# Two-bank PSUM tiles split into one tile per bank, casts moved off ScalarE, a transpose left out, late row tiles routed one by one

## The chip, the cores and the metric

The kernel runs on one core of one Trainium2 chip. The time is the device time of one execution in microseconds (us). Engines are named as the profile names them: PE (TensorE, matmul), PEld (its weight load), DVE (VectorE), ACT (ScalarE), POOL (GpSimd), SP (SyncE, which here only issues DMAs).

## The reference

A gated linear attention over 4 batches, 8 heads, 768 steps and head size 48 is followed by a mixture of 8 experts over the 3072 rows that come out of it. Cut to what is computed:

```python
for t in range(S):
    state = alpha[:, :, t, :, None] * state + einsum('bhd,bhe->bhde', k[:, :, t], v[:, :, t])
    y[:, :, t] = einsum('bhd,bhde->bhe', q[:, :, t], state)
x = y.transpose(0, 2, 1, 3).reshape(3072, 384)
compute = x @ w_skip > 0
e_idx = argmax(x @ w_gate);  gate = softmax(x @ w_gate)[e_idx]
for e in range(8):                      # w1[e]: 384 x 1024, w2[e]: 1024 x 384
    out[rows of e] = x + gate * (relu(x @ w1[e]) @ w2[e])     # only where compute
```

## The kernel before, in words

**Attention.** The rows are cut into 24 tiles of 128, numbered i; two batches go side by side, so i = 2 x chunk + batch within a pair, with 6 chunks per batch. Per tile, DVE scans the decays (L232, L240), POOL multiplies q and k by them (L236, L242), PE makes the scores (L257), DVE copies the masked diagonal blocks (L266) and ACT the others (L272). PE adds the products with v and with the carried state in ps_y (L313); a tiny ACT copy, the fence "spot" (L344), orders two halves of these. ACT copies the result out (turn_y, L351); PE turns it into rows and logits (L359), ACT copies the rows (L365), DVE reduces the logits (L370). PE transposes k (turn_k, L280), ACT copies that, and outer (L293) adds k times v to the state, which DVE scales (L300) and ACT keeps (L305). The last chunk of a batch has no outer, since no chunk follows.

**Routing.** Row tiles are routed in groups. `route` finds the expert and the gate with a string of small DVE instructions and an exp on ACT; ACT rounds the gate into `vals` (L410), POOL subtracts for the low part (L411). `rank` counts rows before each row by two matmuls with the constant matrices tri and one_b (L417, L419), `place` makes slot numbers (L433 to L436). A one-hot of a tile (`one_hot`, L445, 256 columns) times `mv` (`marks`, L450) adds row numbers and gates to a table in PSUM (L458), from which rows are gathered by number.

**Late tiles.** For tiles 18 to 23 the rows of expert 0 do not go through DRAM: one-hots of expert 0's slots (`mine`, L440) select them by matmul (`late_rows`, L509) from two-part splits of the tile (`late_split`, L500, L501) straight into three PSUM banks; `early_turn` (L515) adds the rows gathered earlier, `first_turn` (L523, L525) copies the sum out as xh and xl.

**Experts.** Every matmul is made of two-part operands (hi and lo). Weights come by DMA (L536) as `raw`; ACT casts hi (L556), DVE or POOL subtract for lo (L560). `up(e, g)`, g = 0 to 3, is 18 matmuls into one PSUM bank of three that are taken in turn (ps_y's two and ps_g); ACT makes hh (L633) and DVE hl (L634) from it. `down(e, j)`, j = 0, 1, is 24 matmuls (L645) into ps_v or ps_c; DVE makes o (L649), POOL scatters it by row number (L651). Behind the first down stands `turn(e + 1)`: three transposes into each bank of ps_s (L609), ACT's xh (L611) and DVE's xl (L612) for each. POOL gathers the rows of later experts (L478). A guard checks alpha's range with two ACT instructions (`over`, L597) per down, for eight parts of alpha.

**Order.** The order on each engine is that of the program text (a manual schedule); the framework adds the semaphores from the tiles that instructions read and write. Instructions on one engine run in order. w1's hi and lo have one buffer each, raw has three.

## Time and profile before

| | |
|---|---|
| median of 3 runs (lowest, highest) | 324.94 us (324.41, 328.82) |
| profiled execution, device time | 327.61 us |
| its span in the trace | 325.9 us |
| PE busy | 270.8 us, 83% of the span |
| DVE, POOL, ACT busy | 198.2, 179.2, 159.5 us |
| mean granted PE clock | 0.954 |

The span is what the trace covers; the rest of the device time lies around it. Attention fills the first 136 us, the first up of expert 0 starts at 143.9, the last down ends at 319.3. A row of a timeline gives the start, the length, the engine and line, the operation, what it writes and reads, how many instructions it merges, and in brackets how long the engine was idle before and which instruction ended that. The granted clock is a share of 2.4 GHz.

### The profile page before, as it was taken

What the parts mean: (1) busy time and instruction counts of PE and PEld (TensorE: products, weight loads), DVE (VectorE), ACT (ScalarE), POOL (GpSimd) and SP (SyncE); (2) the same over time, 40 slices, a digit from 0 to 9 for tenths busy, and PEclk for the clock granted to TensorE, in tenths of its full rate; (3) what the DMA queues carried; (4) which work ended last, traced back from release to release, by engine and by line L of the source; (5) the groups of instructions that cost most, each with busy time, mean ns of one, the idle gap of its engine ahead of it and who ended that gap; (6) DMA issues with size and microseconds to landing.
All of it is one profiled execution on the core that took longest, in us unless ns stands there. A gap on an engine that the chain in (4) does not pass through costs nothing.

```text
span 325.9 us, 9204 instructions
## 1 busy us (share of the span) xinstructions
PE 270.8 (83%) x3766; PEld 250.9 (77%) x3766; DVE 198.2 (61%) x362; ACT 159.5 (49%) x338; POOL 179.2 (55%) x199
## 2 busy tenths in 40 slices
PE   0798999898889799893989886878897888898891
PEld 0687987787778688683989886878887888898791
DVE  5765788778778886574555534535438456563720
ACT  3144554545456545612447385495495554453500
POOL 4545564648778978761574552643736265542611
PEclk9998999889999979996799997997999999999998
DMA  7987688969888964713372539449259557250001
GB/s 255 353 309 227 189 271 294 299 209 330 286 250 258 318 202 148 246 54 109 114 251 70 211 90 392 144 162 394 84 186 350 193 171 251 65 195 26 10 12 34
DMA packets 32178, 65.30 MB, mean 200 GB/s; under 512 B 4469, under 2 KB 11535, under 8 KB 32128
## 3 DMA queue, kind: packets, MB, share of 16 engines
q1 hardware_dynamic: 29952, 59.59, 54.9%
q0 software_dynamic: 2176, 5.05, 4.8%
q8 instruction: 31, 0.51, 0.6%
q14 instruction: 19, 0.16, 0.2%
HBM read 56.99 MB, written 8.85 MB: 202 GB/s over the span
## 4 chain that ended last, share of the span: by engine, by line
PE 59%; DVE 13%; ACT 8%; POOL 7%; issue 7%; DMA 3%; SPq 1%; POOLq 0%; DVEq 0%; ACTq 0%
PE ps_y L629 12%; PE ps_c L645 10%; PE ps_y L313 7%; PE ps_v L645 6%; PE ps_g L629 5%; PE ps_s L257 5%; PE ps_g L359 3%; PE ps_k L280 3%; ACT over L597 3%; DVE sfx L240 2%; PE ps_v L458 2%; PE ps_v L293 2%; ACT w1h L556 2%; PE ps_s L609 2%; DVE hl L634 2%
## 5 line engine op out<-in xcount | busy, mean ns | idle before, releaser
L257 PE MATMUL ps_s<-qka 64*64 64x128 f32 (+1 forms) x768 | 33.5, 270 | 11.1 <-DVE qka L242 7.8
L313 PE MATMUL ps_y<-st,vt 64*48 64x128 f32 (+1 forms) x768 | 36.7, 260 | 6.6 <-ACT spot L344 6.1
L560 POOL TENSOR_TENSOR w1l<-raw,w1h 128x512 fp32r<-128x512 f32 x24 | 31.3, 1305 | 17.0 <-ACT w1h L556 13.5
L629 PE MATMUL ps_y<-xh,w1h 128*128 128x240 f32 x132 | 25.3, 300 | 17.1 <-DVE hl L634 16.8
L242 POOL TENSOR_TENSOR qka<-qka,sfx 128x512 f32<-128x512 f32 x23 | 29.4, 1279 | 17.6 <-DVE sfx L240 12.8
L236 POOL TENSOR_TENSOR qka<-qka,pfx 128x512 f32<-128x512 f32 x24 | 26.3, 1095 | 21.1 <-DVE pfx L232 7.9
L651 POOL DMA_INDIRECT out_dram<-o,ids x16 | 17.6, 1098 | 36.9 <-DVE o L649 31.7
L257 PEld LDWEIGHTS ps_s<-qka 64*64 64x64 f32 x768 | 27.0, 143 | 12.4 <-POOL st L160 7.8
L560 POOL TENSOR_TENSOR w2l<-raw,w2h 128x512 fp32r<-128x512 f32 x16 | 21.2, 1327 | 27.1 <-ACT w2h L556 25.9
L629 PEld LDWEIGHTS ps_y<-xh,w1h 128*128 128x128 f32 x132 | 20.4, 205 | 18.8 <-DVE hl L634 18.4
L313 PEld LDWEIGHTS ps_y<-st,vt 64*48 64x48 f32 x768 | 26.8, 129 | 8.9 <-ACT spot L344 7.1
L272 ACT COPY st<-ps_s 64x512 f32<-64x512 f32 x24 | 13.9, 579 | 36.8 <-DVE st L266 30.4
L633 ACT ACTIVATE hh<-ps_y 128x480 fp32r<-128x480 f32 x22 | 12.5, 570 | 38.9 <-PE ps_y L629 35.7
L634 DVE SCALAR_TENSOR_TENSOR hl<-ps_y,hh 128x480 fp32r<-128x480 f32 x22 | 14.4, 652 | 28.1 <-ACT hh L633 28.1
L560 DVE TENSOR_TENSOR w2l<-raw,w2h 128x512 fp32r<-128x512 f32 x32 | 29.3, 935 | 2.8 <-ACT w2h L556 2.2
L232 DVE TENSOR_TENSOR_SCAN pfx<-qka,ps_c 128x527 f32<-128x527 f32 x24 | 29.6, 1233 | 2.2 <-DMA qka<-in_qka_dram 2.2
L240 DVE TENSOR_TENSOR_SCAN sfx<-qka,ps_c 128x525 f32<-128x525 f32 x24 | 29.7, 1238 | 0.3
L266 DVE COPY_PREDICATED st<-mask,ps_s 128x512 f32<-128x512 uint8 x24 | 17.5, 731 | 17.7 <-PE ps_s L257 16.2
L478 POOL DMA_INDIRECT xr<-out_dram,ids x18 | 20.0, 1110 | 13.4 <-DVE gates L495 7.7
L556 ACT CAST w1h<-raw 128x512 fp32r<-128x512 f32 x48 | 27.3, 619 | 0.0
L556 ACT CAST w2h<-raw 128x512 fp32r<-128x512 f32 x48 | 27.1, 616 | 0.0
L629 PE MATMUL ps_y<-xh,w1l 128*128 128x240 f32 x132 | 24.3, 293 | 0.0
(143 smaller groups left out, 711.8 us busy)
## 6 DMA issues: line engine op xcount, KB each, us to landing
raw<-in_w_dram SPq DMA_DIRECT2D x64, 384.0 KB, 5.0
qka<-in_qka_dram SPq DMA_DIRECT2D x48, 256.0 KB, 4.5
qka<-in_qka_dram SPq DMA_DIRECT2D x24, 263.5 KB, 4.2
vt<-in_v_dram SPq DMA_DIRECT2D x24, 192.0 KB, 4.6
out_dram<-x SPq DMA_DIRECT2D x24, 192.0 KB, 4.3
alpha<-in_nat_dram SPq DMA_DIRECT2D x8, 576.0 KB, 4.6
out_dram<-xr SPq DMA_DIRECT2D x6, 192.0 KB, 5.0
xr<-out_dram,ids POOLq DMA_INDIRECT x18, 3.5
```

The source lines that it names most:

```text
L232: nc.vector.tensor_tensor_scan(pfx[:, 0:DEC], dec, self.floor.to_broadcast([P, DEC]), FLOOR, ALU.mult, ALU.max)
L236: nc.gpsimd.tensor_tensor(w["qh"], w["qh"], pfx.rearrange("p (a w) -> p a w", w=SEG)[:, :, 1:P + 1], ALU.mult)
L240: nc.vector.tensor_tensor_scan(sfx[:, 2:DEC][:, ::-1], dec[:, 2:DEC][:, ::-1], self.floor.to_broadcast([P, DEC - 2]), FLOOR, ALU.mult, ALU ...
L242: (eng or nc.gpsimd).tensor_tensor(w["kh"], w["kh"], sfx.rearrange("p (a w) -> p a w", w=SEG)[:, :, 2:P + 2], ALU.mult)
L257: ins = self.nc.tensor.matmul(self.ps[t, r, o:o + (HP if s else P)], lhsT=kh[a, p, t], rhs=qh[a, p, s * HP:], start=True, stop=True, skip_ ...
L313: return self.nc.tensor.matmul(self.py[HP * c:HP * c + D, p % 2, o:o + n], lhsT=lhsT, rhs=rhs, start=first, stop=True, skip_group_check=True)
L478: return [self.nc.gpsimd.indirect_dma_start(out=xr[:n, j, :], out_offset=None, in_=self.out[:, :], in_offset=bass.IndirectOffsetOnAxis(ap= ...
L556: nc.scalar.copy(out=hi[:, s], in_=raw[:, s])
L560: eng.tensor_tensor(lo[:, s], raw[:, s], hi[:, s].bitcast(F32), ALU.subtract)
L629: nc.tensor.matmul(ps[:, u, :], lhsT=a[:, k, f * P:(f + 1) * P], rhs=b[:, k, :], start=(n == 0), stop=(n == len(order) - 1), skip_group_ch ...
L634: nc.vector.scalar_tensor_tensor(out=hl, in0=ps, scalar=0.0, in1=hh.bitcast(F32), op0=ALU.max, op1=ALU.subtract)
L645: nc.tensor.matmul(ps[:r], lhsT=a[:, f, js], rhs=b[:, f, :], start=(n == 0), stop=(n == 3 * FT - 1), skip_group_check=True)
```

## The change

It has four parts.

1. The two-bank tiles ps_s and ps_y are made in pools of the attention stage, and end with it. The expert stage makes four one-bank tiles in their place: ps_x (two, for the turn) and ps_h (two, which with ps_g are the banks of up).
2. The casts of tri and one_b go from the end of iteration 1 to the end of iteration 2; the copy and subtraction of `vals` go from ACT and POOL to DVE.
3. `turn_k` is left out for the last chunk of a batch (i = 10, 11, 22, 23).
4. The late groups are now (18 to 20), 21, 22 and 23. The first is routed by DVE within iteration 21, the others by `route_one`, five small DVE instructions. All their one-hots and `marks` are DVE's, the gating of the six tiles is done once, and the rank of tile 23 is put together from three terms.

The diff, cut to its core:

```diff
     def banks(self, st):
-        self.ps = pp.tile([P, 2, 512], F32, name="ps_s")
-        self.py = pp.tile([P, 2, 512], F32, name="ps_y")
...
     def attention_pools(self, st):
+        both = lambda name: st.enter_context(tc.tile_pool(name=name, bufs=1, space=PSUM))
+        self.ps = both("ps_b").tile([P, 2, 512], F32, name="ps_s")
+        self.py = both("ps_d").tile([P, 2, 512], F32, name="ps_y")
...
-        nc.scalar.copy(out=self.tri, in_=tri_f)
-        nc.scalar.copy(out=self.one_b, in_=self.ones)
+        self.rank_casts = [(self.tri, tri_f), (self.one_b, self.ones)]
...
     def turn_k(self, i):
-        if i >= NT:
+        if i >= NT or self.chunk(i) == C - 1:
...
-    def route(self, g, adder=None):
+    def route(self, g, late=False):
...
+        if not late:
+            yield from self.gating(g, mx)
...
+    def route_one(self, i):
+
+        nc = self.nc
+        t1 = lambda name, w=1: self.sm.tile([P, w], F32, name=name)
+        mx, sk, m2, e1 = self.lmx[:, i - LATE, :], t1("sk"), t1("m2_1"), t1("e1_1", E)
+        L = self.logit[:, i, 0:E]
+        nc.vector.tensor_reduce(out=mx, in_=L, op=ALU.max, axis=AX.X)
+        nc.vector.tensor_scalar(out=sk, in0=self.logit[:, i, E:E + 1], scalar1=0.0, scalar2=None, op0=ALU.is_gt)
+        nc.vector.scalar_tensor_tensor(out=e1, in0=L, scalar=mx, in1=self.rev[:, 0, :], op0=ALU.is_equal, op1=ALU.mult)
+        nc.vector.tensor_reduce(out=m2, in_=e1, op=ALU.max, axis=AX.X)
+        nc.vector.scalar_tensor_tensor(out=self.m[:, i, :], in0=e1, scalar=m2, in1=sk.to_broadcast([P, E]),
+                                       op0=ALU.is_equal, op1=ALU.mult)
+
+    def gating(self, g, mx):
+        nc = self.nc
+        g0, g1 = g
+        n = g1 - g0
+        d, ex = (self.sm.tile([P, GT, E], F32, name=name)[:, :n, :] for name in ("d", "ex"))
+        s1 = self.sm.tile([P, GT, 1], F32, name="s1")[:, :n, :]
+        yield nc.vector.tensor_tensor(d, self.logit[:, g0:g1, 0:E], mx.to_broadcast([P, n, E]), ALU.subtract)
+        yield nc.scalar.activation(out=ex, in_=d, func=AF.Exp)
         yield nc.vector.tensor_reduce(out=s1, in_=ex, op=ALU.add, axis=AX.X)
         yield nc.vector.tensor_scalar(out=s1, in0=s1, scalar1=1e-9, scalar2=None, op0=ALU.add)
         yield nc.vector.reciprocal(self.gate[:, g0:g1, :], s1)
-        nc.scalar.copy(out=self.vals[:, g0:g1, 2:3], in_=self.gate[:, g0:g1, :])
-        nc.gpsimd.tensor_tensor(self.vals[:, g0:g1, 3:4], self.gate[:, g0:g1, :],
-                                self.vals[:, g0:g1, 2:3].bitcast(F32), ALU.subtract)
-
-    def rank(self, g):
+        yield nc.vector.tensor_copy(self.vals[:, g0:g1, 2:3], self.gate[:, g0:g1, :])
+        yield nc.vector.tensor_tensor(self.vals[:, g0:g1, 3:4], self.gate[:, g0:g1, :],
+                                      self.vals[:, g0:g1, 2:3].bitcast(F32), ALU.subtract)
...
+    def rank(self, g, terms=None):
+        pr = self.ranks(g)
+        if terms is None:
+            terms = (self.one_b, self.cnt[:, g0:g1, :]), (self.tri, self.m[:, g0:g1, :])
+        for lhsT, rhs in terms:
+            self.nc.tensor.matmul(pr, lhsT=lhsT, rhs=rhs, start=False, stop=True, skip_group_check=True)
...
     def marks(self, g):
-        self.nc.gpsimd.tensor_tensor(self.mv[:, g0:g1], self.m[:, g0:g1, :].unsqueeze(3).to_broadcast([P, n, E, 4]),
+        (self.nc.vector if g0 >= LATE else self.nc.gpsimd).tensor_tensor(self.mv[:, g0:g1], self.m[:, g0:g1, :].unsqueeze(3).to_broadcast([P, n, E, 4]),
...
-        self.ps_x = bank((self.ps[:, 0, :], self.ps[:, 1, :]), DM)
-        self.ps_h = bank((self.py[:, 0, :], self.py[:, 1, :], self.pg), 2 * ROOM)
+        px = st.enter_context(tc.tile_pool(name="ps_x", bufs=1, space=PSUM))
+        ph = st.enter_context(tc.tile_pool(name="ps_h", bufs=1, space=PSUM))
+        self.ps_x = bank([px.tile([P, 512], F32, name=f"ps_x{n}") for n in range(2)], DM)
+        self.ps_h = bank([ph.tile([P, 512], F32, name=f"ps_h{n}") for n in range(2)] + [self.pg], 2 * ROOM)
...
-        groups = [(0, 6), (6, 12), (12, 18), (18, 22), (22, 24)]
+        groups = [(0, 6), (6, 12), (12, 18), (18, 21), (21, 22), (22, 23), (23, 24)]
...
+                if i == 21:
+                    for _ in self.route(groups[3], True):
+                        pass
                 if i == 22:
+                    self.rank(groups[3])
                     self.table_add()
-                    self.early_rows()
-                    early = self.route(groups[3], nc.vector)
-                    advance(early, 7)
+                    ids = self.numbers(self.tab[:, :, 0:1, :], "ids0", 1)
+                    self.route_one(21)
+                    for _ in self.place(groups[3]):
+                        pass
+                    for t in range(18, 21):
+                        self.mine(t, nc.vector)
                 tick({18: 9}.get(i, 2))
                 if i > LATE:
                     self.late_split(i - 1)
+                if i == 22:
+                    self.early_rows(ids)
                 if i == 1:
                     self.rank_constants()
+                if i == 2:
+                    for out, src in self.rank_casts:
+                        nc.scalar.copy(out=out, in_=src)
...
-            self.rank(groups[3])
-            for _ in self.place(groups[3]):
-                pass
-            for t in range(*groups[3]):
-                self.mine(t, nc.gpsimd)
...
+
+            def put(g):
+                placed[g] = self.place(g)
+                next(placed[g])
+
+            self.rank(g21)
+            self.late_rows(18, range(KT))
+            put(g21)
+            self.mine(21, nc.vector)
+            self.route_one(22)
+            nc.vector.tensor_tensor(self.cnt[:, 22, :], self.cnt[:, 21, :], self.m[:, 21, :], ALU.add)
+            self.late_split(22)
+            self.late_rows(19, range(KT))
             self.rows(b)
             self.logits(b)
             self.row_copy(b)
-            last = self.route(groups[4], nc.vector)
-            advance(last, 7)
-            self.late_split(a)
+            self.rank(g22, [(self.one_b, self.cnt[:, 22, :]), (self.tri, self.m[:, 22, :])])
+            self.rank(g23, [(self.one_b, self.cnt[:, 22, :]), (self.one_b, self.m[:, 22, :])])
+            self.route_one(b)
+            put(g22)
+            self.mine(a, nc.vector)
             self.late_split(b, nc.vector)
-            self.late_rows(18, range(KT))
-            self.rank(groups[4])
-            for t in (19, 20):
+            for t in (20, 21):
                 self.late_rows(t, range(KT))
-            for n, _ in enumerate(self.place(groups[4])):
-                if n == 0:
-                    for t in (a, b):
-                        self.mine(t, nc.vector)
-            self.late_rows(21, range(KT))
+            self.rank(g23, [(self.tri, self.m[:, b, :])])
+            put(g23)
+            self.mine(b, nc.vector)
             self.early_turn()
             for t in (a, b):
                 self.late_rows(t, range(KT))
+            for g in groups[4:]:
+                advance(placed[g])
+            gates = self.gating((LATE, NT), self.lmx)
+            advance(gates, 2)
+            for t in range(18, 21):
+                self.one_hot(t, nc.vector)
             self.first_turn()
-            for t in range(18, NT):
-                self.one_hot(t, nc.gpsimd if t % 2 else nc.vector)
-            advance(early, 99)
-            advance(last, 99)
-            for g in groups[3:]:
-                self.marks(g)
+            advance(gates, 99)
+            self.marks((LATE, NT))
+            for t in range(21, NT):
+                self.one_hot(t, nc.vector)
+            for t in (a, b):
+                nc.vector.tensor_tensor(self.cnt[:, t + 1, :], self.cnt[:, t, :], self.m[:, t, :], ALU.add)
             self.store(a)
```

What this does to the order of instructions is shown at three places. A row has the line, the operation, what it writes and reads, the shape and the semaphores of other engines that it waits for (DMASW and DMAHW are DMA queues); a number behind a tile's name tells tiles of one name apart.

**PE, the second and third up of expert 0 and the turn of expert 1.** xh_2451 and xh_2460 are the same operand in the two kernels. Before:

```order
L629 MATMUL ps_y<-xh_2451,w1h 128x240 [waits DVE_49]
L629 MATMUL ps_y<-xh_2451,w1h 128x240 x2
L629 MATMUL ps_y<-xh_2451,w1l 128x240 x3
L629 MATMUL ps_g<-xh_2451,w1h 128x240 x3
...
L609 MATMUL ps_s<-ident,xr_2502 128x128 [waits DMASW2_49]
L609 MATMUL ps_s<-ident,xr_2502 128x128 x2
L609 MATMUL ps_s<-ident,xr_2502 128x112 [waits DMASW3_49,DVE_49]
L609 MATMUL ps_s<-ident,xr_2502 128x112 x2
```

And with the change:

```order
L659 MATMUL ps_h_2509<-xh_2460,w1h 128x240 x3
L659 MATMUL ps_h_2509<-xh_2460,w1l 128x240 x3
L659 MATMUL ps_g<-xh_2460,w1h 128x240 x3
...
L659 MATMUL ps_h_2508<-xh_2460,w1h 128x240 [waits DVE_49]
L659 MATMUL ps_h_2508<-xh_2460,w1h 128x240 x2
...
L639 MATMUL ps_x_2506<-ident,xr_2511 128x128 [waits DMASW2_49]
L639 MATMUL ps_x_2506<-ident,xr_2511 128x128 x2
L639 MATMUL ps_x_2507<-ident,xr_2511 128x112 [waits DMASW3_49]
L639 MATMUL ps_x_2507<-ident,xr_2511 128x112 x2
```

The second up and the second half of the turn no longer wait for DVE. The fourth up (ps_h_2508 for the second time) waits for DVE's hl of the first.

**DVE, from the routing of the last tile to the last `mine`.** `mine` is a one-hot of expert 0's slots, latel the low part of a tile's split, sl a slot number. Before:

```order
L370 TENSOR_REDUCE ps_c<-ps_g 128x9 [waits PE_49]
L395 TENSOR_REDUCE mx<-ps_c 128x2 [waits DVE_49]
L396 TENSOR_TENSOR ps_c<-ps_c,mx 128x16 [waits DVE_49]
L397 TENSOR_TENSOR ps_c<-ps_c,rev 128x16 [waits DVE_49]
L398 TENSOR_REDUCE m_2378<-ps_c 128x2 [waits DVE_49]
L399 TENSOR_TENSOR eq<-ps_c,m_2378 128x16 [waits DVE_49]
L400 SCALAR_TENSOR_TENSOR m<-ps_c,eq 128x16 [waits DVE_49]
L403 TENSOR_TENSOR cnt<-cnt,m 128x8 [waits DVE_49] x2
L404 TENSOR_TENSOR d<-ps_c,mx 128x16
L501 TENSOR_TENSOR latel_2395<-x,lateh_2394 128x384 [waits Activation_49]
L433 SCALAR_TENSOR_TENSOR sl<-ps_v,m 128x16 [waits PE_49]
L440 TENSOR_SCALAR mine_2421<-slots,sl 128x240 [waits DVE_49]
L440 TENSOR_SCALAR mine_2423<-slots,sl 128x240
```

And with the change:

```order
L371 TENSOR_REDUCE ps_c<-ps_g 128x9 [waits PE_49]
L416 TENSOR_REDUCE lmx<-ps_c 128x1 [waits DVE_49]
L417 TENSOR_SCALAR sk<-ps_c 128x1
L418 SCALAR_TENSOR_TENSOR e_1_2395<-ps_c,lmx,rev 128x8 [waits DVE_49]
L419 TENSOR_REDUCE m_1_2394<-e_1_2395 128x1 [waits DVE_49]
L420 SCALAR_TENSOR_TENSOR m<-e_1_2395,m_1_2394,sk 128x8 [waits DVE_49]
L461 SCALAR_TENSOR_TENSOR sl_2401<-ps_v,m 128x8 [waits PE_49]
L469 TENSOR_SCALAR mine_2404<-slots,sl_2401 128x240 [waits DVE_49]
L529 TENSOR_TENSOR latel_2407<-x,lateh_2406 128x384 [waits Activation_49]
L461 SCALAR_TENSOR_TENSOR sl_2423<-ps_v,m 128x8 [waits PE_49]
L469 TENSOR_SCALAR mine_2426<-slots,sl_2423 128x240 [waits DVE_49]
```

The routing of tiles 22 and 23 together (seven rows and two counts) has become that of tile 23 alone; the one-hot of tile 22 now stands ahead of the split, and each `mine` has its own wait for PE's rank. Those of tiles 18 to 21 have come from POOL and stand ahead of these rows.

**ACT, around the end of iteration 1.** spot is the fence of the next iteration. Before:

```order
L365 COPY x<-ps_g 128x384 [waits PE_49]
L282 COPY kt<-ps_k 128x512 [waits PE_49]
L172 CAST tri<-tri_f 128x128 [waits Pool_49]
L174 CAST one_b<-ones_f 128x128
L344 COPY spot<-ident 1x1 [waits PE_49,Activation_49]
```

And with the change:

```order
L366 COPY x<-ps_g 128x384 [waits PE_49]
L283 COPY kt<-ps_k 128x512 [waits PE_49]
L345 COPY spot<-ident 1x1 [waits PE_49,Activation_49]
...
L283 COPY kt<-ps_k 128x512 [waits PE_49]
L977 CAST tri<-tri_f 128x128 [waits Pool_49]
L977 CAST one_b<-ones_f 128x128
L345 COPY spot<-ident 1x1 [waits PE_49,Activation_49]
```

The casts stand ahead of the fence of iteration 3 instead of that of iteration 2.

## Rows read from the trace of the kernel before

**Rows 1.** Four stretches: us, busy us of PE, PEld, DVE, ACT, POOL, then PEclk.

```profile
0.00:136.00 136.00, 115.91 (x2695) 101.04 (x2697) 101.12 (x204) 65.64 (x161) 90.25 (x121) 0.96 0.82 261
149.00:159.00 10.00, 6.84 (x33) 6.73 (x33) 4.47 (x10) 2.46 (x5) 2.10 (x2) 0.50 0.42 137
168.40:173.00 4.60, 4.60 (x28) 4.58 (x29) 1.88 (x2) 4.07 (x8) 2.15 (x2) 1.00 0.39 142
193.10:215.80 22.70, 19.00 (x127) 18.52 (x126) 10.55 (x15) 14.16 (x26) 11.03 (x9) 0.92 0.62 221
```

**Rows 2.** Waits of PE from 146 us on: total, times, longest us.

```profile
PE ps_y L629 <- DVE hl L634: 16.8, 9, 3.2
...
PE ps_s L609 <- DVE xl L612: 8.1, 7, 1.2
```

**Rows 3.** The chain of waits from 100 us on: start, us, what.

```profile
153.91 4.20 PE ps_y L629 x18
...
160.66 2.02 PE ps_y L629 x18
162.68 4.19 PE ps_c L645 x24
...
199.70 3.90 PE ps_y L629 x18
...
308.61 2.29 PE ps_y L629 x18
...
319.31 0.63 DVE o L649
```

**Rows 4.** Timeline of PE, expert stage, with the idle time before.

```profile
148.39 2.35 PE L458 MATMUL ps_v<-mv,hot 128*128 128x32 f32 x12 [2.21 <-POOL mv L450]
153.91 1.00 PE L629 MATMUL ps_y<-xh,w1h 128*128 128x240 f32 x3 [3.16 <-DVE hl L634]
...
168.36 0.51 PE L609 MATMUL ps_s<-ident,xr 112*128 112x112 f32 x3 [1.16 <-DVE xl L612]
...
199.70 0.49 PE L629 MATMUL ps_y<-xh,w1h 128*128 128x240 f32 x2 [2.53 <-DVE hl L634]
```

**Rows 5.** Timeline of PE at a fence in the attention loop.

```profile
27.75 0.66 PE L313 MATMUL ps_y<-st,vt 64*48 64x64 f32 x16 [1.52 <-ACT spot L344]
```

**Rows 6.** Timeline of ACT at two casts ahead of fences.

```profile
27.11 0.30 ACT L172 CAST tri<-tri_f 128x128 bf16<-128x128 f32 x1 [2.14 <-POOL tri_f L169]
...
61.94 0.20 ACT L410 CAST vals<-gate 128x6 fp32r<-128x6 f32 x1 [2.52 <-DVE gate L409]
```

**Rows 7.** The chain of waits from 60 to 100 us, keys' turn.

```profile
74.91 0.51 PE ps_k L280 x4
```

**Rows 8.** Timelines of POOL, DVE and ACT around the late tiles.

```profile
136.47 3.52 POOL L440 TENSOR_SCALAR mine<-slots,sl 128x240 fp32r<-128x240 f32 x4
...
123.39 1.81 DVE L445 TENSOR_SCALAR hot<-slots,s 128x256 fp32r<-128x256 f32 x2
...
127.35 0.20 DVE L370 TENSOR_REDUCE ps_c<-ps_g 128x9 f32<-128x36 f32 x1 [1.50 <-ACT x L365]
...
127.73 0.60 DVE L445 TENSOR_SCALAR hot<-slots,s 128x256 fp32r<-128x256 f32 x2
...
143.48 0.36 ACT L523 CAST xh<-ps_s 128x240 fp32r<-128x240 f32 x1 [5.41 <-PE ps_s L509]
```

**Rows 9.** Timeline of POOL at the first gathers of the experts.

```profile
156.30 1.11 POOL L478 DMA_INDIRECT xr<-out_dram,ids  x1 [7.71 <-DVE gates L495]
157.72 0.99 POOL L478 DMA_INDIRECT xr<-out_dram,ids  x1 [0.30 <-issue]
```

**Rows 10.** Timeline of ACT, casts and guard instructions in a down.

```profile
189.29 1.15 ACT L556 CAST w1h<-raw 128x512 fp32r<-128x512 f32 x2
190.33 1.26 ACT L597 ACTIVATE over<-alpha,lim 128x1152 bf16<-128x1152 f32 x1
...
191.71 1.26 ACT L597 ACTIVATE over<-alpha,lim 128x1152 bf16<-128x1152 f32 x1
```

More of the change, by code (lines that the diff above doesn't have):

```diff
@@ L182, in rank_constants @@
         self.gate = const.tile([P, NT, 1], F32, name="gate")
+        self.lmx = const.tile([P, NT - LATE, 1], F32, name="lmx")
     def slot_constants(self):
@@ L392, in route @@
         bc = lambda a: a.to_broadcast([P, n, E])
-        mx, d, ex, m2, s1, eq = t1("mx"), t("d"), t("ex"), t1("m2"), t1("s1"), t("eq")
+        mx = self.lmx[:, g0 - LATE:g1 - LATE, :] if late else t1("mx")
+        m2, eq = t1("m2"), t("eq")
         e0, e1 = (a[:, :n, :] for a in self.p6[:2])
@@ L402, in route @@
         for i in range(g0, g1):
-            (adder or nc.gpsimd).tensor_tensor(self.cnt[:, i + 1, :], self.cnt[:, i, :], self.m[:, i, :], ALU.add)
-        yield nc.vector.tensor_tensor(d, L, bc(mx), ALU.subtract)
-        nc.scalar.activation(out=ex, in_=d, func=AF.Exp)
-        yield
+            (nc.vector if late else nc.gpsimd).tensor_tensor(self.cnt[:, i + 1, :], self.cnt[:, i, :], self.m[:, i, :],
+                                                             ALU.add)
+        if not late:
[19 more added lines that the diff above has]
+        yield nc.scalar.activation(out=ex, in_=d, func=AF.Exp)
         yield nc.vector.tensor_reduce(out=s1, in_=ex, op=ALU.add, axis=AX.X)
@@ L409, in route, with ranks @@
         yield nc.vector.reciprocal(self.gate[:, g0:g1, :], s1)
-        nc.scalar.copy(out=self.vals[:, g0:g1, 2:3], in_=self.gate[:, g0:g1, :])
-        nc.gpsimd.tensor_tensor(self.vals[:, g0:g1, 3:4], self.gate[:, g0:g1, :],
-                                self.vals[:, g0:g1, 2:3].bitcast(F32), ALU.subtract)
-    def rank(self, g):
-        g0, g1 = g
-        pr = self.pv[:, TR:TR + (g1 - g0) * E].rearrange("p (n e) -> p n e", e=E)
-        self.nc.tensor.matmul(pr, lhsT=self.one_b, rhs=self.cnt[:, g0:g1, :], start=False, stop=False,
-                              skip_group_check=True)
-        self.nc.tensor.matmul(pr, lhsT=self.tri, rhs=self.m[:, g0:g1, :], start=False, stop=True,
-                              skip_group_check=True)
+        yield nc.vector.tensor_copy(self.vals[:, g0:g1, 2:3], self.gate[:, g0:g1, :])
+        yield nc.vector.tensor_tensor(self.vals[:, g0:g1, 3:4], self.gate[:, g0:g1, :],
+                                      self.vals[:, g0:g1, 2:3].bitcast(F32), ALU.subtract)
+    def ranks(self, g):
+        o = TR + max(0, g[0] - LATE) * E
+        return self.pv[:, o:o + (g[1] - g[0]) * E].rearrange("p (n e) -> p n e", e=E)
+    def rank(self, g, terms=None):
+        g0, g1 = g
+        pr = self.ranks(g)
[3 more added lines that the diff above has]
+            self.nc.tensor.matmul(pr, lhsT=lhsT, rhs=rhs, start=False, stop=True, skip_group_check=True)
     def place(self, g):
@@ L426, in place @@
         n = g1 - g0
-        pr = self.pv[:, TR:TR + n * E].rearrange("p (n e) -> p n e", e=E)
-        sl = self.sm.tile([P, GT, E], F32, name="sl")[:, :n, :]
-        s2 = self.late.tile([P, GT, 1], F32, name=f"s{g0}")[:, :n, :]
+        pr = self.ranks(g)
+        sl = self.late.tile([P, n, E], F32, name=f"sl{g0}")
+        s2 = self.late.tile([P, n, 1], F32, name=f"s{g0}")
         for i in range(g0, g1):
@@ L435, in place @@
         yield nc.vector.tensor_reduce(out=s2, in_=sl, op=ALU.add, axis=AX.X)
-        yield nc.vector.memset(pr, 0.0)
+        if g0 < LATE:
+            yield nc.vector.memset(pr, 0.0)
     def mine(self, i, eng):
@@ L481, in fetch_rows, with early_rows @@
             bounds_check=N - 1, oob_is_err=False) for j, n in enumerate((P, LAST))]
[L483 to L484 removed]
+    def early_rows(self, ids):
         for ins in self.fetch_rows(self.xr0, ids, 0):
@@ L940, in static_path @@
             self.x0begun = set()
-            self.rank(groups[3])
-            for _ in self.place(groups[3]):
-                pass
-            for t in range(*groups[3]):
-                self.mine(t, nc.gpsimd)
+            g21, g22, g23 = groups[4:]
+            placed = {}
+            def put(g):
[9 more added lines that the diff above has]
+            self.late_rows(19, range(KT))
             self.rows(b)
```

2 lines of the change are left out of this document (removed).

## The prediction

> **What bounds the kernel now.** I read the stretches first, then the waits of TensorE (PE) in the expert stage, then the chain of waits to see what lies on the path, and last the timelines where PE stands still.
>
> PE is busy 115.9 of the first 136 us and, in the third expert, 19.0 of 22.7 [rows 1]. It is the bound nearly everywhere, so time goes where it idles or runs slowly. In the expert stage it waits 16.8 us in 9 pieces for hl and 8.1 us in 7 pieces for xl, both from VectorE (DVE) [rows 2]. Both have one cause: ps_y and ps_s are one tile of two banks each, so matmuls into one bank wait until DVE has read the other. The chain [rows 3] shows these waits on the path, and also what undisturbed work costs: 2.02 for an up of 18 matmuls, 4.19 for a down of 24. Nine ups that begin behind such a wait are longer, from 4.20 (the first) to 2.29 (the last); the one at 199.70 took 3.90. In 149 to 159 the granted clock was 0.50, that is 1.2 GHz, and from 168.4 to 173 it was 1.00, 2.4 GHz [rows 1]; PE idled 2.21 and 3.16 in the first stretch, 2.53 ahead of 199.70, and only 1.16 ahead of 168.36 [rows 4]. So long waits are paid twice, once as idle and once as slow matmuls.
>
> Between attention and experts PE waits 2.21 for mv, computes the table in 2.35, and waits 3.16 for hl [rows 4]. In the attention loop it waits for the fence "spot" on ScalarE (ACT), 1.52 at 27.75 [rows 5]. ACT stood there 2.14 at the cast of tri, which waited for POOL and is queued ahead of the fence; at 61.94 it stood 2.52 at vals, waiting for the gate, and alike in the next group of tiles [rows 6].
>
> **The change part by part**, against the profiled execution: span 325.9, device time 327.61. The median of the runs shown is 324.94, so 2.67 comes off at the end.
>
> *Casts off ACT.* One iteration later the cast of tri finds tri_f done; of the 1.52 some 0.2 remains, since two casts still precede a fence. Gain 1.3, between 0 and 1.5. The vals copy and subtraction become two DVE instructions per group, 0.2 each like the small reduction at 127.35 [rows 8]. The two fences of the later groups no longer wait for the gate, but DVE itself is late there and holds the causal copy. I take 0.5 for each, with ends 0 and 1.5 (what the fence at 27.75 cost).
>
> *No turn of keys in the last chunk.* Four tiles lose 4 transposes, 0.51 on the chain [rows 7], at most 2.0; where DVE or POOL end the iteration, nothing comes back. I take 0.4. Attention is then 1.3 + 1.0 + 0.4 = 2.7; I use 2.5, with ends 0 and 4.5.
>
> *Late tiles.* Four one-hots on POOL take 3.52; late_rows end at 143.48, where ACT's xh follows them [rows 8]. Now all one-hots of the late tiles are on DVE. One took 0.30 there (two in 0.60 at 127.73), but 0.9 at 123.39 (two in 1.81), where POOL was multiplying [rows 8]. PE now runs two tiles' late_rows ahead of the last tile's rows, and behind these rows DVE has nine small instructions of 0.2, a split, two one-hots and two ranks to wait for. At 0.30 late_rows end near 141.9; at 0.9, with those of tiles 18 to 20 late as well, near 145. POOL issues gathers and splits beside them part of the time, so I take 142.4: gain 1.1, ends -1.5 and 1.5.
>
> The Trainium skill (Perfetto Trace Analysis, Optimizing Scalar/DVE Operations) warns that GpSimd's port is one of DVE's own, so that moving work between these two may not help; by it the 0.9 would hold throughout and this term would be -1.5, the time 2.6 us longer. The pairs at 127.73 and 123.39 agree that a neighbour on POOL matters, but show it only while POOL runs.
>
> *Marks and table.* The gates of all late tiles become one pass of five small DVE instructions, then mv once, on DVE. The idle of 2.21 falls to about 0.75, ends 0.3 and 2.2: gain 1.45. An idle of 1.16 left the clock at 1.00 [rows 1, 4], so the table should take half of its 2.35: gain 1.15.
>
> *Banks of their own.* The order shows the second up and the second half of the turn without DVE's wait. An up then waits only for hl of three ups before, with two other ups, 4.0 us, between. The longest wait for hl was 3.16, so all 16.8 go. The seven for xl (1.16 each) go as well: 8.1; the down behind the turn writes another bank. The ups behind waits, and the one after the first, took together 8.0 more than 2.02 each; that returns if PE doesn't stop.
>
> *What is late next.* (a) Expert 1. The first gather is issued 5.6 us behind the table's end, held by the gates on DVE [rows 4, 9]. With the terms above the table ends at 142.4 + 2.7 (first up, 148.39 - 2.21 - 143.48) + 0.75 + 1.2 = 147.1, the first gather goes at 152.7, and the first down starts three ups behind the table, at 153.3 instead of 162.68: it gains 9.4, the gathers only 3.6. POOL then has six gathers, two parts of w1l and a scatter, each about 1.4 as from 156.30 to 157.72 [rows 9]: the second w1l ends at 165.3. Up(1,0) starts at 162.4 and reads it from 163 on. POOL may be quicker where it finds its operands, so I take a stall of 1.7, ends 0 and 3. (b) ACT in experts 1 to 4. Each down queues two casts (1.15 together) and two guard instructions, 1.38 from one to the next [rows 10]. With hh and xh near a cast's length, an expert asks 12 casts, 4 hh, 2 xh and 4 guards of ACT: 18 x 0.57 + 5.5 = 15.8 of the 17.2 that PE needs (4 x 2.02 + 2 x 4.19 + 0.7 for the turn). Counted from the turn: xh ends at 0.7, two downs' casts and guards (7.8) at 8.5, hh(e+1,0) at 9.1 and its hl at 9.8, before PE wants the bank at 10.2. Three times two casts and an hh (5.2) end at 14.3, the last two casts at 15.4, their lo parts near 16.4, and the first down reads those from 15.7. I take 0.7 in three experts, 2.1, with ends 0 and 12 (four times 3).
>
> **Sum.** 2.5 + 1.1 + 1.45 + 1.15 + 16.8 + 8.1 + 8.0 - 1.7 - 2.1 = 35.3. From 327.61 this leaves 292.3; less 2.67, 289.6. Counted the other way: the first down at 153.3, 9.1 to the end of expert 0, 1.7, six experts of 17.2, a last one of 16.5 and 2.1 end at 285.9, against 319.31 [rows 3], that is 33.4, and 35.9 with attention. The last o and scatter stay. I predict **290 us**.
>
> **The rivals.**
> 1. *ACT takes the place of the banks.* If guards hold hh and the last parts of w2 by their whole 2.8 per down, experts 1 to 4 lose 3 each: 12 - 2.1 = 10 more, 300 us. For it: 14.2 us of ACT in an expert [rows 1] must now fit into 17.2, in a fixed order. Against: PE wants nothing of ACT for two ups. Chance 0.17.
> 2. *The slow clock stays.* The pause ahead of the table, at up(1,0), or one in the guard experts lowers the clock again: 2.2 each (4.20 - 2.02), two or three of them, 294 to 297. For it: the pause of 2.21 stands ahead of a slow table. Chance 0.14.
> 3. *Slower than before.* PE now hops from bank to bank without the long waits, but with a micro-pause at each hop, and the clock could swing through all experts. An up at the low clock costs 2.2 more; from 16 of the 32 ups on (35.3 / 2.2) the gain is gone, and with all of them it is 360 us. Against it: the up at 160.66 passes into the down at 162.68 without a gap, and both have their full-clock length [rows 3]. The Trainium skill (TensorE: Matmul & The Clock Gate, A second HAM failure mode: psum-queue depth-cycling) tells of a kernel whose clock swung because it cycled through PSUM banks; by it the low clock would return in every expert. The trace does not show that so far. Chance 0.02.
> 4. *The banks are still tied.* Were the new tiles tracked together after all, only the terms ahead of the experts count: 327.61 - 6.2 - 2.67 = 319. The order shows these waits gone. Chance 0.02.
>
> The forecast has 0.65 and a range of its own, 283 to 297: attention and late tiles at their lower ends add 5, and 2 more for (a) and the table; at their upper ends, without stalls, they take off 6 to 7. The **range**, 283 to 302, takes in rivals 1 and 2. A measurement of this kernel tells 2%, 6.5 us, from no change, so faster is below 318.4: the forecast and rivals 1 and 2, less a little for a worse rival 1. Faster 0.95, same 0.03, slower 0.02.
>
> **What will show it.** PE waits for hl and xl in the expert stage under 2 us in all, and experts 17.2 to 18.5 apart, the longest being those with guards, where PE waits, if at all, for w1l or w2l. A granted clock of 1.00 from the table on. No cast of tri or vals that waits ahead of a fence. Less than 1 us of idle ahead of the table. The prediction is wrong if experts still take over 19 us, whatever PE then waits for, or if one-hots on DVE push late_rows past 145.

## The result, and the profile after

The changed kernel takes **290.73 us** (289.45 to 291.45, 4 runs) against 326.14 for the kernel before beside it: a ratio of 0.8903, 95% interval 0.8828 to 0.8979. Run again beside the experiments it took 289.63, 0.8881 (0.8840 to 0.8923). The forecast was 290, in a range of 283 to 302. Medians take in all executions of a kernel, while the ratios leave out, on both sides, slow ones (over 1.5% above the fastest of their kernel), so a ratio can differ from that of the medians. The profiled execution took 291.45 with a span of 289.7; the one before had 327.61 and 325.9.

First the waits of PE from 130 us on, in total, times, longest (after; they answer to [rows 2]):

```profile
PE ps_h L659 <- POOL w1l L588: 1.1, 1, 1.1
PE ps_v L487 <- DVE mv L479: 0.4, 1, 0.4
PE ps_h L659 <- ACT xh L551: 0.2, 1, 0.2
```

The 16.8 for hl and 8.1 for xl are gone. What is left is one wait for w1l, 1.1 us in expert 1, 0.4 ahead of the table, where it was 2.21 [rows 4], and 0.2 for xh ahead of the first up, as before. The chain of waits (after; [rows 3]):

```profile
144.26 1.74 PE ps_v L487 x12
146.01 3.41 PE ps_h L659 x18
149.42 2.34 PE ps_g L659 x18
...
164.40 1.73 PE ps_h L659 x13
166.12 2.01 PE ps_g L659 x18
168.14 4.03 PE ps_h L659 x36
172.16 4.19 PE ps_c L675 x24
176.35 0.62 PE ps_x L639 x6
176.97 4.19 PE ps_v L675 x24
181.16 2.02 PE ps_g L659 x18
...
283.37 0.63 DVE o L679
```

The four ups of an expert (8.1 together; the chain merges two of them at 168.14), the first down, six transposes in one piece of 0.62, and the second down follow each other without a gap, except for the wait in expert 1. Counted from first down to first down, expert 1 comes 18.39 behind expert 0, the others 17.05 to 17.37 behind the one before; it was 20.05 to 22.98. The last down ends at 283.37 instead of 319.31.

The stretches (after; us, busy us of PE, PEld, DVE, ACT, POOL, then the granted clock; [rows 1]):

```profile
130.00:136.00 6.00, 6.00 (x52) 5.10 (x52) 3.86 (x17) 1.67 (x4) 4.01 (x4) 0.50 0.71 242
146.00:150.00 4.00, 4.00 (x23) 4.00 (x23) 3.49 (x6) 2.13 (x5) 0.00 (x0) 0.57 0.68 214
181.00:198.20 17.20, 17.20 (x128) 17.15 (x128) 10.86 (x15) 14.21 (x28) 11.64 (x9) 1.00 0.81 291
```

In an expert PE is busy all of 17.2 us, at 2.4 GHz. Two slow stretches at 1.2 GHz are still there: 130 to 136, with the late rows, and 146 to 150, where the second up took 3.41 and the third 2.34 instead of 2.02.

Put together: up(0,0) starts 2.4 us earlier (143.90, now 141.53); from there to the first down 12.08 instead of 18.61; from there to the last down's end 129.7 instead of 156.8. That is 2.4 + 6.5 + 27.0 = 35.9 of the span's 36.2.

### The profile page after: what moved, and what is told of

Its sections match the earlier page's. It is cut to its first block, busy times and chain, and to the rows that moved or that the text cites. A ratio compares the mean times of both kernels' runs of the same rounds, so it can differ in the third digit from the quotient of the medians.

```text
span 289.7 us, 9180 instructions
## 1 busy us (share of the span) xinstructions
PE 260.3 (90%) x3755; PEld 245.0 (85%) x3755; DVE 205.4 (71%) x385; ACT 155.5 (54%) x328; POOL 173.1 (60%) x185
## 4 chain that ended last, share of the span: by engine, by line
PE 69%; DVE 14%; issue 5%; POOL 5%; ACT 3%; DMA 2%; SPq 1%; POOLq 0%; DVEq 0%
PE ps_h L659 15%; PE ps_c L675 10%; PE ps_v L675 10%; PE ps_y L314 8%; PE ps_g L659 7%; PE ps_s L258 5%; PE ps_g L360 5%; DVE sfx L241 3%; PE ps_k L281 2%; DVE st L267 2%; DVE pfx L233 2%; DMA qka<-in_qka_dram 2%; PE ps_v L294 2%; POOL xr L507 1%; ACT xt L352 1%
## 5 line engine op out<-in xcount | busy, mean ns | idle before, releaser
L314 PE MATMUL ps_y<-st,vt 64*48 64x128 f32 (+1 forms) x768 | 38.0, 260 | 3.4 <-ACT spot L345 1.8
L237 POOL TENSOR_TENSOR qka<-qka,pfx 128x512 f32<-128x512 f32 x24 | 26.3, 1094 | 18.2 <-DMA qka<-in_qka_dram 6.4
L507 POOL DMA_INDIRECT xr<-out_dram,ids x18 | 21.1, 1170 | 20.8 <-DMA alpha<-in_nat_dram 16.7
L588 DVE TENSOR_TENSOR w2l<-raw,w2h 128x512 fp32r<-128x512 f32 x32 | 31.1, 991 | 1.6 <-ACT w2h L584 1.5
L314 PEld LDWEIGHTS ps_y<-st,vt 64*48 64x48 f32 x768 | 27.6, 128 | 5.3 <-ACT spot L345 2.0
L588 POOL TENSOR_TENSOR w2l<-raw,w2h 128x512 fp32r<-128x512 f32 x16 | 21.9, 1371 | 16.8 <-ACT w2h L584 16.8
L267 DVE COPY_PREDICATED st<-mask,ps_s 128x512 f32<-128x512 uint8 x24 | 17.6, 734 | 11.6 <-PE ps_s L258 10.2
L588 DVE TENSOR_TENSOR w1l<-raw,w1h 128x512 fp32r<-128x512 f32 x24 | 23.3, 979 | 2.7 <-ACT w1h L584 2.5
L360 PE MATMUL ps_g<-xw,xt 112*64 112x105 f32 x384 | 24.5, 273 | 0.0
L659 PE MATMUL ps_h<-xh,w1l 128*128 128x240 f32 x132 | 23.1, 280 | 1.1 <-POOL w1l L588 1.1
L360 PEld LDWEIGHTS ps_g<-xw,xt 112*64 112x64 f32 x384 | 19.4, 145 | 4.8 <-issue 3.3
L659 PE MATMUL ps_h<-xh,w1h 128*128 128x240 f32 x132 | 22.9, 280 | 0.2 <-ACT xh L551 0.2
```

What stands on the lines that cost most here:

```text
L237: nc.gpsimd.tensor_tensor(w["qh"], w["qh"], pfx.rearrange("p (a w) -> p a w", w=SEG)[:, :, 1:P + 1], ALU.mult)
L314: return self.nc.tensor.matmul(self.py[HP * c:HP * c + D, p % 2, o:o + n], lhsT=lhsT, rhs=rhs, start=first, stop=True, skip_group_check=True)
L360: ins = self.nc.tensor.matmul(self.pg[t, p * RW:(p + 1) * RW], lhsT=w["xt"][:PD, p, t], rhs=self.xw[:PD, p, :], start=True, stop=True, ski ...
L507: return [self.nc.gpsimd.indirect_dma_start(out=xr[:n, j, :], out_offset=None, in_=self.out[:, :], in_offset=bass.IndirectOffsetOnAxis(ap= ...
L588: eng.tensor_tensor(lo[:, s], raw[:, s], hi[:, s].bitcast(F32), ALU.subtract)
L659: nc.tensor.matmul(ps[:, u, :], lhsT=a[:, k, f * P:(f + 1) * P], rhs=b[:, k, :], start=(n == 0), stop=(n == len(order) - 1), skip_group_ch ...
```

## The experiments

The runs came in three groups, each on a chip of its own, with the kernel before measured beside it. Its median differed (329.7, 328.2, 326.1), so runs are compared by their ratio to it; 1% is 3.3 us. Unless said otherwise, the changed kernel stands at the 0.8881 of its second measurement.

**Banks alone.** The kernel before with the three hunks on ps_s, ps_y, ps_x and ps_h, and nothing else.

> The kernel before with the first part alone: a tile for each bank in the expert stage. Theory (PE waited in the experts only because two banks were one tile, and each wait was paid twice, as idle and as slow matmuls): the waits for hl and xl vanish, experts stand 17.1 to 18 apart, about 30.5 us less than before (26.7 from the first down to the last one, as in the traces of before and after, and about 4 around the first three ups), 295 to 297 us. Rival (the other parts are needed too: with POOL's one-hots left as they were, the gathers and ACT come too late for the faster experts): waits for w1l or hh take their place, 300 us or more.

299.01 us, 0.9077 (0.9000 to 0.9154): 30 us less than before. The experts are 17.05 to 17.37 apart from the first on, and in them PE waits for nothing but mv (2.21). The theory's size and its place hold (its 295 to 297 was counted from a kernel before at 326); the rival does not, since no wait for w1l or hh takes the place of the others. Expert 1 has not even the 1.07 of the changed kernel: POOL issues the first gather 2.7 us ahead of the first down (162.90 and 165.63), there 2.0 (151.63 and 153.61). That lead comes back below.

**All but the banks.**

```diff
-        self.ps_h = bank([ph.tile([P, 512], F32, name=f"ps_h{n}") for n in range(2)] + [self.pg], 2 * ROOM)
+        pht = ph.tile([P, 2, 512], F32, name="ps_h")
+        self.ps_h = bank([pht[:, n, :] for n in range(2)] + [self.pg], 2 * ROOM)
```

and the same for ps_x.

> The changed kernel, but with ps_h and ps_x again as one tile of two banks each. Theory: the waits for hl and xl come back in all experts; only the gain ahead of the experts stays, 319 to 323 us. Rival (the waits were due to late casts and splits, which the other parts relieve): below 300 us.

322.23 us, 0.9811 (0.9727 to 0.9894), 6 us less than before. The waits of PE (this kernel; total, times, longest) are back, within 0.1 of [rows 2]:

```profile
PE ps_h L661 <- DVE hl L666: 16.9, 9, 3.2
...
PE ps_x L641 <- DVE xl L644: 8.2, 7, 1.2
```

30 and 6 make the 36 of the whole change, so the parts add up within intervals of about 3 us each.

**The turn's banks tied, the others apart.** The hunk on ps_x alone is undone.

> The changed kernel, but with the two banks of the turn (ps_x) as one tile again; ps_h stays apart. Theory: seven waits of 1.16 us for xl come back and nothing else, since an idle of 1.16 did not lower the clock: 8 us more than the changed kernel, 298 to 299.5 us. Rival 1 (the waits only move later stalls): 291 to 294. Rival 2 (each of the seven pauses also lowers the clock): 8 more plus 7 times about 4 for a down at the low clock, over 310 us.

302.44 us, 0.9202 (0.9126 to 0.9277): 10 us more than the changed kernel, two more than expected. Six experts are 18.4 to 18.7 apart, about 1.4 more than in the changed kernel. From the start of the first down to that of the second it takes 6.12 instead of 4.74, that is 1.38 more for a wait of 1.16, so 0.2 is lost beside the wait. The clock was 1.00 from 175 to 286, against rival 2. The seventh wait, in expert 0, was 6.4 us:

```profile
PE ps_x L640 <- DVE xl L643: 13.4, 7, 6.4
```

xl stands on DVE behind o(0,0), and o waits 6.5 for the gather of expert 0's rows. That wait is in the changed kernel too (5.0 ahead of o at 161.10), only PE doesn't see all of it.

**Late tiles as before.** Banks, casts and keys' turn changed, routing and one-hots of the late tiles not.

> The kernel before with banks, casts and keys' turn changed, but the late tiles routed in two groups with their one-hots on POOL as before. Theory (the late part is worth what the sum had for it, 1.1 + 1.45 + 1.15): 3.7 us more than the changed kernel, 294 to 295 us. Rival (one-hots on DVE only move the wait, and the routing of tiles 18 to 20 holds PE in iteration 21): 290 us or less, no worse than the changed kernel.

296.29 us, 0.8982 (0.8915 to 0.9048), 3.3 us more than the changed kernel at 0.8881; the intervals just overlap. The size fits the sum; the rival's "290 or less" is out. But this kernel has no stall in expert 1, which comes 17.05 behind expert 0, so the 3.3 is what the late part gains ahead of the experts less what expert 1 gives back.

**The one-hots back on GpSimd.** Four calls of `self.mine(.., nc.vector)` take `nc.gpsimd`.

> The changed kernel with the six one-hots of expert 0's slots (mine) on GpSimd again, everything else as changed. Theory (on VectorE one takes 0.3 there, since GpSimd mostly issues DMAs beside it, against 0.9 on GpSimd): late_rows end 2 to 4 us later, counted from the rows of tile 21, and the whole is 2 to 4 us above the changed kernel. Rival (the two engines share what they read through, so the move gained nothing): no difference.

294.08 us, 0.9014 (0.8961 to 0.9067): 4.3 us more, just above the theory's 2 to 4; "no difference" is out. In the timelines (start, length, idle time before), first the changed kernel's three on DVE, then this kernel's on POOL and PE's wait for the fourth:

```profile
130.98 0.84 DVE L469 TENSOR_SCALAR mine<-slots,sl 128x240 fp32r<-128x240 f32 x3
```

```profile
130.76 2.60 POOL L469 TENSOR_SCALAR mine<-slots,sl 128x240 fp32r<-128x240 f32 x3 [4.30 <-DVE sl L461]
...
134.49 1.27 POOL L507 DMA_INDIRECT xr<-out_dram,ids  x1 [0.17 <-issue]
...
137.24 0.90 POOL L469 TENSOR_SCALAR mine<-slots,sl 128x240 fp32r<-128x240 f32 x1
```

```profile
138.19 0.57 PE L537 MATMUL ps_s<-mine,lateh 128*128 128x240 f32 x1 [2.86 <-POOL mine L469]
```

0.28 each on DVE, 0.87 on POOL. On POOL they also stand ahead of the gather at 134.49 and the last ones behind it, so PE waits 2.86.

**Guards twice.**

```diff
-                for j, scale in enumerate((-1.0, 1.0)):
+                for j, scale in [(0, -1.0), (1, 1.0)] * 2:
```

> The changed kernel with each guard instruction issued twice: 8 instead of 4 on ScalarE per expert from the second down of expert 0 to the first of expert 4, 5.5 us more ScalarE work in an expert. Theory (ScalarE's order has slack for four guards, and that is why the 2.1 us of the prediction did not come): by the prediction's own count hh of the next expert's first up ends 5.5 later, at 14.6 from the turn, and its hl at 15.3, where PE wants the bank at 10.2, so three experts take 22 to 23.5 us and the whole is 15 to 19 us above the changed kernel. Rival (ScalarE has far more slack than counted, PE needs nothing of it): 0 to 3 us more.

311.39 us, 0.9502 (0.9434 to 0.9570), 20 us more. The first downs of experts 1 to 5 are 18.4, 23.6, 24.4, 22.8 and 20.0 us behind the one before, and PE (this kernel's timeline) waits for hl:

```profile
185.47 1.00 PE L659 MATMUL ps_g<-xh,w1h 128*128 128x240 f32 x3 [3.45 <-DVE hl L664]
...
209.84 0.99 PE L659 MATMUL ps_h<-xh,w1h 128*128 128x240 f32 x3 [4.01 <-DVE hl L664]
```

So the count of ACT's queue is right in kind: with four guards hh comes just in time, with eight it holds PE. The rival falls. The whole is a little above the theory's 15 to 19, which had no slow clock: behind these two waits the granted clock was 0.50 (185 to 190 and 209 to 215), and the two ups took 4.20 and 4.19 instead of 2.02.

**Casts back** (tri and one_b at the end of iteration 1; the early groups' vals on ACT and POOL) and **keys' turn back** (`if i >= NT:`).

> The changed kernel, but with the casts of tri and one_b back at the end of iteration 1 and, for the three early groups, the copy of vals on ScalarE and the subtraction on GpSimd again. Theory, from the traces: the cast of tri costs 1.9 us between the rows of tiles 0 and 1 (6.1 apart instead of 4.2), while the casts of vals cost nothing, since VectorE is late in those iterations with either: about 1.9 us more. Rival (the prediction's sum): 1.3 for tri and 0.5 for each of two vals, 2.3 us more, with iterations 8 and 14 about 0.5 longer each.

> The changed kernel, but with the turn of keys in the last chunk put back (4 transposes and one copy in each of 4 tiles, whose result nobody reads). Theory (PE ends the iteration in about one of the four): 0.4 us more, not to be told from the changed kernel. Rival (PE ends it in all four): 2.0 us more, 0.7%.

292.07 us, 0.8811 (0.8732 to 0.8891), and 291.21 us, 0.8860 (0.8808 to 0.8912): neither can be told from the changed kernel. For the keys' turn that is what the theory said, and the rival's 0.7% is not seen. For the casts it is inconclusive: the wait is there (this kernel, PE),

```profile
26.78 1.10 PE L315 MATMUL ps_y<-st,vt 64*48 64x64 f32 x16 [2.04 <-ACT spot L346]
```

and the rows of tiles 0 and 1 begin 6.95 apart instead of 4.24, but attention as a whole varies more: the rows of the last tile begin between 129.1 and 135.6 us in five executions with the changed loop.

**Three orders that aim at what is left.** First the routing of tiles 18 to 20 goes behind `self.causal(i + 1)` of iteration 22, and the gather of expert 2 behind the downs of expert 0:

```diff
-                if i == 21:
+                if i == 22:                      # now right behind self.cross(i + 1)
                     for _ in self.route(groups[3], True):
...
-                if e + 2 < E:
+                if e and e + 2 < E:
                     self.gather(e + 2)           # and self.gather(2) behind the downs of e == 0
```

> The changed kernel with two instructions' places changed: the routing of tiles 18 to 20 on VectorE behind the causal copy of tile 23 instead of ahead of it, and the gather of expert 2 behind the downs of expert 0. Theory (both waits that the changed kernel's trace still shows ahead of expert 2, 1.29 us of PE for the turn of iteration 22 and 1.07 for w1l in expert 1, come from work queued ahead of what PE waits for): both go, the slow clock behind the first goes with it, expert 1 begins 17.1 behind expert 0: 2 to 4.5 us less than the changed kernel. Rival (the waits move: VectorE's chain up to the one-hots of the late tiles is as long as before): less than 1.3 us, the part of expert 1 alone.

290.33 us, 0.8857 (0.8808 to 0.8905): no difference. The pause of 1.29 is not in its trace, but not in that of the second execution of the changed kernel either (below); expert 1 still waited 0.97 for w1l and came 18.3 behind. The theory falls. The rival's size holds, though not even the part that it granted came; and expert 2 now comes 18.2 behind expert 1, where it was 17.1, which may be the price of its later gather (not tested apart). Then the split itself goes ahead of the scatter that it stood behind:

```diff
+                if e == 0:
+                    advance(splits, 2)
                 if e + 2 < E:
                     self.gather(e + 2)
...
-                    advance(splits, 2)           # behind each down
+                    if e or j:
+                        advance(splits, 2)
```

> The changed kernel with the routing of tiles 18 to 20 behind the causal copy of tile 23 and two splits of w1 of expert 1 ahead of the first down of expert 0 instead of behind it. Theory (PE waited for w1l in expert 1 because that split stood on GpSimd behind a scatter whose o waited for the gather of expert 0's own rows): the wait goes, expert 1 begins 17.1 behind expert 0 instead of 18.3; with the other move 1 to 3 us less than the changed kernel. Rival (the gathers themselves are late): the wait of about 1 us stays, as xl or xr.

288.29 us, 0.8832 (0.8799 to 0.8864), 1.6 us less than the changed kernel; the intervals overlap. PE no longer waits for w1l, but 0.90 for xr and 0.72 for xl; expert 1 comes 19.2 behind, not 17.1. That is the rival's wait: the gathers themselves are late. The theory is not all wrong: in this execution the second up ran at full clock, and the changed kernel's expert 1 came 22.3 to 22.4 behind in the two executions where it did so (below). DVE's timeline (this kernel) shows what is left:

```profile
160.48 0.62 DVE L679 SCALAR_TENSOR_TENSOR o<-ps_c,gates,xr 128x384 f32<-128x384 f32 x1 [6.03 <-DMA xr<-out_dram,ids]
161.02 0.96 DVE L642 TENSOR_TENSOR xl<-ps_x,xh 128x384 fp32r<-128x384 f32 x2
```

o waits 6.03 for the rows of expert 0 and xl stands behind it. The last kernel therefore issues the gathers earlier: on DVE the table's sum, row numbers and gates go ahead of hl(0,0), and the three memsets of xr go to POOL.

```diff
+        if between:                              # in up, behind the matmuls of (0, 0)
+            between()                            # last_table, gather(1), gather(0)
...
-            self.nc.vector.memset(t, 0.0)
+            self.nc.gpsimd.memset(xr, 0.0)       # in gather, for the first three
```

> The kernel x10_split_first, and the table's sum, row numbers and gates on VectorE ahead of hl of the first up, with the three memsets of xr on GpSimd, each ahead of its gather. Theory: the gathers are issued about 3 us earlier and hl(0,0) 2 us earlier, nothing of expert 0 or 1 waits, but what was left to gain there is gone with x10 already: within 0.5 us of it. Rival (the slow clock behind the table comes from PE's pause and is independent of both): up(0,1) at 3.4 in one, 2.0 in the other by chance, 1.5 to 2.5 us between them.

**284.43 us**, 0.8705 (0.8669 to 0.8740): faster than both kernels, 2.0% below the changed one beside it by their ratios. My theory, that nothing was left to gain, falls. So does the rival's price: the second up ran at full clock in this execution and in that of the kernel it was made from, and still there are 3.9 us between their medians. POOL's timeline of the changed kernel and of this one:

```profile
151.63 1.22 POOL L507 DMA_INDIRECT xr<-out_dram,ids  x1 [16.71 <-DMA alpha<-in_nat_dram]
...
154.87 1.03 POOL L507 DMA_INDIRECT xr<-out_dram,ids  x1 [0.30 <-issue]
```

```profile
142.50 0.74 POOL L608 MEMSET xr<- 128x768 f32 x1 [9.55 <-PE ps_v L487]
143.58 1.04 POOL L507 DMA_INDIRECT xr<-out_dram,ids  x1 [0.33 <-POOL xr L608]
...
146.94 1.03 POOL L507 DMA_INDIRECT xr<-out_dram,ids  x1 [0.27 <-POOL xr L608]
```

The table began at 144.26 there and at 140.56 here: the first gather is issued 3.0 us behind it instead of 7.4, that of expert 0's own rows 6.4 instead of 10.6. Expert 1 begins 17.05 behind expert 0, and behind the table (0.45 ahead of it) PE waits for nothing.

**The changed kernel again.**

> The changed kernel itself once more, as the measure for the other runs beside it: 289 to 292 us, 0.885 to 0.895 of before.

289.63 us, within the expected range. Its trace differs from the first one where the code is the same. The clock (this execution; columns as above) was 1.00 in both places where the first was slow:

```profile
126.00:136.00 10.00, 9.00 (x128) 8.04 (x117) 8.35 (x40) 3.56 (x10) 4.30 (x4) 1.00 0.51 179
139.00:147.00 8.00, 8.00 (x70) 7.92 (x69) 6.69 (x17) 5.13 (x10) 0.90 (x1) 1.00 0.47 147
```

but PE then waited longer for expert 1 (this execution's timeline):

```profile
152.03 0.51 PE L639 MATMUL ps_x<-ident,xr 112*128 112x112 f32 x3 [0.88 <-DMA xr<-out_dram,ids]
159.61 0.38 PE L659 MATMUL ps_h<-xh,w1l 128*128 128x240 f32 x1 [2.33 <-POOL w1l L588]
```

From up(0,0) to the first down of expert 1 it took 32.9 us, with the slow clock early 30.5, and 27.5 in the last kernel above. The first gather was issued only 0.4 us ahead of the first down here (146.10 and 146.47), 2.0 in the first execution, 4.7 in the last kernel above (143.58 and 148.29).

The other traces say the same. Six executions have the changed kernel's order up to expert 1: these two and those of the runs with one-hots, casts and keys' turn back and with doubled guards. In four the second up was slow; the lead of the gather was 2.0, and expert 1 came 18.2 to 18.5 behind expert 0. In the other two (this one and keys' turn back) the second up took 2.0; the lead was 0.4, and expert 1 came 22.4 and 22.3 behind. With a lead of 2.6 and more (late tiles as before, banks alone, the last kernel) it came 17.05 behind. So the gathers set when expert 1 can go on. A fast clock ahead of the first down shortens their lead, and more than it gains is lost again: in a longer wait, and here in a granted clock of 0.63 behind the 2.33 (159.6 to 164).

## Why the prediction was right, step by step

Both profiled executions of the changed kernel are set against the one trace of the kernel before. Up to the last o the traces themselves have 35.9 and 39.1; what follows it took 6.6 us before, 6.3 in the first and 7.8 in the second.

| step | predicted gain | first execution | second |
|---|---|---|---|
| start, up to the rows of tile 0 | not counted | 2.5 | 3.0 |
| attention, on to the rows of tile 21 | 2.5 | 1.8 | 3.3 |
| late tiles, on to the first up | 1.1 | -2.0 | 1.6 |
| idle ahead of the table | 1.45 | 1.76 | 1.76 |
| table | 1.15 | 0.6 | 0.6 |
| waits for hl, xl | 16.8 + 8.1 | 16.8 + 8.1 | 16.8 + 8.1 |
| ups behind waits | 8.0 | 6.3 | 8.0 |
| behind the seven turns (0.22 each) | not counted | 1.5 | 1.5 |
| expert 1 | -1.7 | -1.3 | -5.3 |
| guards | -2.1 | 0 | 0 |
| sum, up to the last o | 35.3 | 36.1 | 39.4 |

The main step, banks, was right in cause and size, and the runs with banks alone and with all but banks show it: 30 of the 36 us. The other 6 came out near their sum by luck: terms missed on both sides, and the two executions reach it by different ways.

*Start.* The rows of tile 0 begin at 19.67 instead of 22.21, though none of the four parts stands ahead of them. From 17 us on PE ran the same instructions faster, as the four transposes of keys for tile 1 show (before, then after), with a granted clock of 1.00 in both profiles:

```profile
17.59 1.12 PE L280 MATMUL ps_k<-ident,qka 128*128 128x128 f32 x4
```

```profile
17.20 0.66 PE L281 MATMUL ps_k<-ident,qka 128*128 128x128 f32 x4
```

The cause stays open. This makes up all of the 2.4 us by which the first up came earlier; attention and late tiles, with 1.8 and -2.0, cancel.

*Attention.* The cast of tri gave 1.9 (rows of tiles 0 and 1 are 4.24 apart, before 6.12), not 1.3; in this pair that is all of attention's gain. The vals gave nothing: tiles 13 to 15 are 10.4 apart, before 10.5; the term of 0.5 each was too large, since DVE ends those iterations.

*Late tiles.* Between the rows of tile 21 and the end of late_rows lie 15.6 us, before 13.6: the term of 1.1 failed in this pair. The one-hots are fast, but the routing of tiles 18 to 20 stands on DVE ahead of a causal copy, PE pauses 1.29 while that is late, and the clock is low behind the pause (0.50 from 130 to 136):

```profile
128.79 0.66 PE L314 MATMUL ps_y<-qka,state 64*48 64x128 f32 x16 [1.29 <-ACT xt L352]
```

In the second execution the same code has neither and took 12.0. So the term was -2.0 in one and 1.6 in the other, both past its ends of -1.5 and 1.5; what brings the pause in one and not in the other is not shown.

The Trainium skill's warning (Perfetto Trace Analysis, Optimizing Scalar/DVE Operations) that GpSimd and DVE share a port would have made this term 2.6 worse. Here it did not decide: a one-hot took 0.28 on DVE, and putting them back on GpSimd cost 4.3.

*The slow clock.* The step "returns if PE doesn't stop" failed for one up: PE paused only 0.45 ahead of the table, and still the second up took 3.41 at a granted clock of 0.57 (146 to 150). Rival 2 came true to that extent, but not with its price: where the second up was fast, the first down of expert 1 came 32.7 and 32.9 us behind up(0,0), and in the four executions where it was slow 30.3 to 30.6.

*Guards.* This step failed by a wrong place in the queue. I put the last two casts of w2 behind the fourth hh. They stand behind the third; the fourth is followed by w1 of the next expert. ACT, then DVE, around the ups of expert 4 (after; its turn ended at 211.13):

```profile
218.94 0.55 ACT L663 ACTIVATE hh<-ps_h 128x480 fp32r<-128x480 f32 x1
...
222.37 1.14 ACT L584 CAST w2h<-raw 128x512 fp32r<-128x512 f32 x2
223.47 0.57 ACT L663 ACTIVATE hh<-ps_h 128x480 fp32r<-128x480 f32 x1
223.93 1.13 ACT L584 CAST w1h<-raw 128x512 fp32r<-128x512 f32 x2
```

```profile
219.52 0.66 DVE L664 SCALAR_TENSOR_TENSOR hl<-ps_h,hh 128x480 fp32r<-128x480 f32 x1 [2.40 <-ACT hh L663]
...
224.43 1.22 DVE L588 TENSOR_TENSOR w2l<-raw,w2h 128x512 fp32r<-128x512 f32 x1
```

hl of the first up ends at 220.18, 9.0 from the turn (9.8 predicted, wanted at 10.2), and the last part of w2 on DVE at 225.65, 14.5 from it, where 16.4 was predicted and 15.7 is the limit. So nothing waits, and the run with doubled guards shows how near the limit is.

*Expert 1.* The size was near in the first execution by luck, and the reason only half right. The sum took ups at full clock, which gave a first gather 0.6 us ahead of the first down, and a stall of 1.7, at most 3. The second execution has these ups and a lead of 0.4, and expert 1 lost 5.3: its 22.4 us are past the 19 that I had named as a sign of being wrong. The first lost 1.3 only because a slow second up left the gathers more time. I had POOL's queue as the limit. It is the gathers: the w1l stands behind a scatter, that behind o, and o behind the gather of expert 0's own rows.

*Rival 3* did not come. In the first execution PE changes banks 48 times in the ups and downs without a wait at the change, other than the first for xh, and the mean granted clock from 152 to 283 us is 1.00. What the Trainium skill tells of psum-queue depth-cycling (TensorE: Matmul & The Clock Gate, A second HAM failure mode: psum-queue depth-cycling) does not show in this kernel.

## What to carry to other kernels

Where an engine waits for readers of a buffer that it is not about to write, look at what the framework tracks: two banks in one tile are one buffer. A wait that vanishes moves the next consumer forward and leaves its other inputs where they were; list for each who must now be earlier (here the gathers), and shorten their chain in the same change. Count a queue by its actual order, instruction by instruction. Set a second execution beside the first before calling a term right: here a total held in both while its terms changed sign.
